# Attention and routed experts on one core: attention's transfers queued in written order, the routing noise later, and filler matmuls on TensorE

## The chip, the core and the metric

The kernel runs on one core of one Trainium2 chip. The metric is the device time of one execution in microseconds (us); lower is better. A core has five engines, each of which takes its own instructions strictly in the order in which they were queued: TensorE (PE, matmuls into PSUM; its weight loads are listed as PEld), VectorE (DVE), ScalarE (ACT), GpSimd (POOL) and SyncE (SP), which here issues nearly all transfers. The engines meet only at semaphores: an instruction whose input is not there stops everything queued behind it on its engine.

## What is computed

The program is a chain of three layers over 2304 tokens (4 sequences of 576) of width 512.

```python
# attention: q, k, v (4, 8, 576, 64); p (4, 8, 32, 64)
p_packed = softmax(p @ k.T / 8) @ v            # 32 packed rows for each sequence and head
x = softmax(q @ p_packed.T / 8) @ p_packed     # (2304, 512) after the heads are put together
# routing: 8 experts, two for each token
noisy = x @ w_gate + log1p(exp(x @ w_noise)) * noise
top2, weights = two_largest(noisy), softmax_of_the_two
# experts, d = 512, f = 1024
x2[token] = sum over its two experts of weight * (relu(x @ w1[e]) @ w2[e])
# dense layer, 512 -> 2048 -> 512
h = x2 @ w_in;  out = (h * sigmoid(h)) @ w_out
```

## The kernel before

The sequence of stages is attention (from 0 to about 118 us of the profile), then the eight experts, then the dense layer; from the first expert matmul on, TensorE has nearly always something to do.

**Attention** is worked off in 16 slots. `packed(b, g)` makes the packed rows of sequence `b` and head group `g` (eight units; `START1` gives the slot in which each begins), `unpacked(t, n, lg)` applies them to `n` token tiles of 128 rows from tile `t` on (ten units, u0 to u9; `START2`). Each unit is a generator of four steps, and `slot_steps` calls the steps that are due. In a unit of the first kind TensorE turns k (`kp`, `krp`), multiplies by p (`s`, L362 and L365), turns the exponentials (`ap`, `apr`) and multiplies by v (`pp`). In one of the second kind it turns q (`qp`), makes scores (`s`, L429 and L436), turns the normalised exponentials (`a2p`) and makes rows of x (`xp`), which ACT copies to `xr` and SP stores to DRAM (`xs`). The normalising multiplication (`sd` <- `sd`, `mx`) is GpSimd's, and stands between the exponentials and `a2p`.

**Routing** is done in two parts. `route(0, 11, ...)` takes the first 11 tiles as soon as u5 has made tile 10; it is a chain of small VectorE operations with two exchanges with ScalarE, and ends in `idx`, the list of the rows that expert 0 reads first. GpSimd fetches these rows with two indirect DMAs (`xg`, L196), TensorE turns them (`tps`), and the first expert matmul (`hps`, L208) follows. Tiles 11 to 17 (u6 to u9) are routed while expert 0 already computes.

**Weights of expert 0** are eight pieces (`wa0` to `wa7`) of 512 KB. Each is loaded to one of three buffers (`raws`), then `split` makes the two parts that the fast matmul format wants: ScalarE writes `wa?h`, GpSimd writes the remainder `wa?l` in four pieces.

```python
def split(hi, lo, src, eng=V):
    pin(A.activation(hi, src, AF.Copy))
    parts = 4 if eng is G else 1
    for i in range(parts):
        s = slice(i * 1024 // parts, (i + 1) * 1024 // parts)
        eng.tensor_tensor(lo[:, s], src[:, s], hi[:, s].bitcast(F32), op=OP.subtract)
```

**What sets the order.** The code is traced by a scheduler that orders each engine's instructions by its own estimate of when they can run, so an instruction may end up ahead of others that were written earlier; `tc.keep_in_program_order` takes that freedom away for the instructions given to it. The slot in which a piece of weights is asked for is `START1[i] + WLOAD` (slots 4, 5, 6, 7, 8, 8, 11 and 12), its split comes two slots later. SP has eight semaphores for its transfers, so a transfer is issued only when the eighth before it has landed.

Of the kernel before, what the change touches and what calls it, by code (L numbers as in the profile page):

```python
# [32 lines left out]
WLOAD = 4  # L33
# [11 lines left out]
def body(ctx: ExitStack, tc: tile.TileContext, q, k, v, p, wg, wn, noise, w1, w2, w_in, w_out, out):  # L45
# [58 lines left out]
    M = {"pin": False, "w": 384, "hb": 3}  # L104
# [26 lines left out]
    def load(dst, src, c, eng=V, runs=False):  # L131

        hi, lo = dst
        raw = raws.tile([P, 1024], F32, name="raw", tag="raw")
        if runs:
            for b in range(4):
                nc.sync.dma_start(raw[32 * b:32 * b + 32].rearrange("j (a f) -> j a f", a=4),
                                  src[b * P:(b + 1) * P].rearrange("(a j) f -> j a f", a=4))
        else:
            nc.sync.dma_start(raw.rearrange("p (c f) -> p c f", c=c), src.rearrange("(c p) f -> p c f", p=P))  # L140
        later.append(lambda: split(hi, lo, raw, eng))
# [93 lines left out]
    def expert_block(e, j0, n, x):  # L235
# [3 lines left out]
        def step2(f, h):  # L239
# [3 lines left out]
            if f == 7:  # L243
                for j, y in enumerate(acc[0]):
                    ysb = M["s"].tile([P, DM], F32, name="ysb", tag="ysb", bufs=3)
                    cp(A if j % 2 else V, ysb, y)
                    i = j0 + j
                    r0 = (e * TA + i if i < TA else E * TA + e * TB + i - TA) * P
                    nc.sync.dma_start(ys[r0:r0 + P, :], ysb)
# [8 lines left out]
    with ExitStack() as ax:  # L258
# [14 lines left out]
        def load_kv(nm, b, g):  # L273
            src = {"k": k, "v": v}[nm]
            m = wa.tile([P, 1024], F32, name=f"{nm}m", tag=f"wa{2 * b + g}{'hl'[nm == 'v']}")
            m = m.rearrange("p (h r) -> p h r", h=4)
            nc.sync.dma_start(m, src[b, 4 * g:4 * g + 4, 0:512, :].rearrange("h (p r) d -> p h (r d)", r=4))
# [6 lines left out]
        def load_q(b):  # L284
            for g in range(2):
                m = xp_.tile([P, 4 * BW], F32, name="qm", tag=f"x{'hl'[g]}{'ab'[b % 2]}")
                m = m[:, 0:1024].rearrange("p (h r) -> p h r", h=4)
                nc.sync.dma_start(m, q[b, 4 * g:4 * g + 4, 0:512, :].rearrange("h (p r) d -> p h (r d)", r=4))
# [4 lines left out]
            nc.sync.dma_start(qt["r", b // 2][o:o + 64], q[b, :, 512:576, :].rearrange("h p d -> p h d"))  # L293
# [12 lines left out]
        pd = sk.tile([P, 9, 64], F32, name="pd", bufs=1)  # L306
        nc.sync.dma_start(pd[:, 0:8, :], p.rearrange("b (g j) k d -> (j k) (b g) d", g=2))
# [6 lines left out]
        nc.sync.dma_start(wgn[0:64, :, 0:8], wg.rearrange("(h d) e -> d h e", h=H))  # L314
        nc.sync.dma_start(wgn[0:64, :, 8:16], wn.rearrange("(h d) e -> d h e", h=H))
# [25 lines left out]

        def packed(b, g):
# [66 lines left out]
        def unpacked(t, n, lg):  # L409
# [45 lines left out]
            for i in range(n):  # L455
# [11 lines left out]
                nc.sync.dma_start(xs[r0:r0 + P, :], xr)  # L467
# [184 lines left out]
        tick()  # L652
        r1 = route(EARLY, NT - EARLY, lgs[EARLY])
# [302 lines left out]
```

## Time and profile before

| what | value |
|---|---|
| time, median of 3 runs | 995.24 us (993.43 to 997.77) |
| the profiled execution's own time | 991.13 us |
| its span in the trace | 989.3 us |
| PE busy | 957.0 us, 97% of the span |
| PEld, DVE, ACT, POOL busy | 821.0, 447.4, 346.4, 313.4 us |
| chain that ended last | PE 90%, DVE 4%, DMA 3%, ACT 1% |

The span is what the trace covers; 1.8 us of the profiled execution lie around it. TensorE is busy nearly throughout, so what a change near the beginning is worth is the time by which it moves the point from which TensorE never waits again, and any matmul that it adds or speeds up.

### The profile page before, as it was taken

The numbers are of one execution on the slowest core, as the hardware profiler recorded it, in microseconds if no ns is written. First come the engines' busy times: TensorE is split into PE (matmuls) and PEld (weight loads), VectorE is DVE, ScalarE is ACT, GpSimd is POOL, SyncE is SP. The second block draws the span as 40 slices with busy tenths as digits, with TensorE's granted clock in tenths as the row PEclk, the third lists the DMA queues.
The fourth block names the chain that finished last, engine by engine and source line by source line (L and its number), as shares of the span: only waits on it lengthen the run. The fifth ranks groups of instructions, "written<-read, shape, count | busy, mean of one in ns | idle before, by whom it ended". The sixth has DMA issues, their size and how long they took to land.

```text
span 989.3 us, 14385 instructions
## 1 busy us (share of the span) xinstructions
PE 957.0 (97%) x5584; PEld 821.0 (83%) x5584; DVE 447.4 (45%) x871; ACT 346.4 (35%) x631; POOL 313.4 (32%) x345
## 2 busy tenths in 40 slices
PE   6989799999999999999999999999999999999996
PEld 4767589899999999998999988888888888888884
DVE  4537763666767576766634557222122221111111
ACT  3567322433434343433323343322222222222221
POOL 2166214343525243443200136333323322222221
PEclk9989899999999999999999999999999999999998
DMA  9994324576757676566623454111011110001001
GB/s 243 249 270 161 107 65 125 188 231 202 231 167 227 188 235 199 189 226 207 188 64 117 149 194 136 54 28 37 22 53 33 32 43 1 1 1 43 0 1 46
DMA packets 82298, 122.49 MB, mean 124 GB/s; under 512 B 16432, under 2 KB 49200, under 8 KB 82224
## 3 DMA queue, kind: packets, MB, share of 16 engines
q1 hardware_dynamic: 74704, 101.58, 32.6%
q0 software_dynamic: 7520, 19.93, 7.0%
q8 instruction: 46, 0.75, 0.3%
q14 instruction: 28, 0.23, 0.1%
HBM read 93.17 MB, written 28.31 MB: 123 GB/s over the span
## 4 chain that ended last, share of the span: by engine, by line
PE 90%; DVE 4%; DMA 3%; ACT 1%; SPq 1%; issue 1%; ACTq 0%
PE hps L208 14%; PE hps L210 14%; PE hps L209 14%; PE acc L219 14%; PE acc L218 14%; PE acc L220 14%; PE xp L460 1%; PE tps L157 1%; PE s L429 1%; PE s L362 1%; DMA vm<-in_v_dram 1%; DMA km<-in_k_dram 1%; DVE rt_oa L534 1%; PE kp L351 0%; DMA raw<-wf_out 0%
## 5 line engine op out<-in xcount | busy, mean ns | idle before, releaser
L176 POOL DMA_INDIRECT xg<-xs,idx x120 | 127.0, 1059 | 195.1 <-DVE xturn L185 147.6
L750 POOL TENSOR_TENSOR gl<-sg,gh 128x512 fp32r<-128x512 f32 (+1 forms) x80 | 95.4, 1194 | 253.5 <-ACT gh L749 237.9
L231 ACT ACTIVATE hh<-hps 128x384 fp32r<-128x384 f32 (+1 forms) x128 | 56.0, 438 | 260.5 <-PE hps L210 256.8
L746 DVE TENSOR_TENSOR sg<-hps,sg 128x512 f32<-128x512 f32 (+1 forms) x80 | 50.7, 634 | 196.2 <-ACT sg L745 196.0
L232 DVE SCALAR_TENSOR_TENSOR hl<-hps,hh 128x384 fp32r<-128x384 f32 (+1 forms) x128 | 62.4, 488 | 122.0 <-ACT hh L231 121.3
L745 ACT ACTIVATE sg<-hps 128x512 f32<-128x512 f32 (+1 forms) x80 | 44.2, 553 | 189.5 <-PE hps L210 189.2
L749 ACT ACTIVATE gh<-sg 128x512 fp32r<-128x512 f32 (+1 forms) x80 | 47.1, 589 | 79.3 <-DVE sg L746 79.1
L736 POOL DMA_INDIRECT y<-ys,slots x36 | 36.7, 1019 | 110.9 <-DVE hl L232 72.4
L739 DVE TENSOR_SCALAR y<-y,gates 128x512 f32<-128x512 f32 x18 | 10.9, 607 | 37.9 <-DMA y<-ys,slots 37.9
L740 DVE SCALAR_TENSOR_TENSOR y<-y,gates,y 128x512 f32<-128x512 f32 x18 | 15.7, 871 | 25.1 <-DMA y<-ys,slots 25.0
L460 PE MATMUL xp<-ppBD,a2T 128*128 128x272 f32 (+1 forms) x80 | 23.5, 433 | 1.6 <-ACT xr L51 0.8
L185 DVE STREAM_TRANSPOSE xturn<-xg 128x512 f32<-128x512 f32 x30 | 21.2, 706 | 3.7 <-DMA wf_in<-t 2.5
L689 DVE SCALAR_TENSOR_TENSOR t<-raw,t 128x512 int32<-128x512 int32 x32 | 22.2, 693 | 0.9
L690 DVE SCALAR_TENSOR_TENSOR t<-raw,t 128x512 int32<-128x512 int32 x32 | 22.1, 691 | 0.9
L196 POOL DMA_INDIRECT xg<-xs,idx x10 | 9.7, 969 | 40.3 <-DVE idx_f L555 19.5
L686 ACT ACTIVATE t<-raw 128x512 f32<-128x512 f32 x32 | 21.2, 662 | 0.1
L208 PE MATMUL hps<-xha,wa3h 128*128 128x256 f32 (+1 forms) x56 | 17.7, 316 | 1.8 <-DVE sg L746 1.8
L160 DVE TENSOR_TENSOR xla<-tps,xha 128x512 fp32r<-128x512 f32 x14 | 9.6, 690 | 21.1 <-ACT xha L159 21.1
L53 DVE COPY ysb<-acc 128x512 f32<-128x512 f32 x24 | 16.4, 682 | 4.9 <-PE acc L220 4.8
L429 PE MATMUL s<-ppT,qT 128*128 128x64 f32 x128 | 17.9, 291 | 0.0
L208 PE MATMUL hps<-xha,wa0h 128*128 128x256 f32 (+1 forms) x56 | 17.6, 314 | 0.2 <-ACT xha L159 0.2
L208 PE MATMUL hps<-xha,wa2h 128*128 128x256 f32 (+1 forms) x56 | 17.7, 316 | 0.1
(450 smaller groups left out, 2976.4 us busy)
## 6 DMA issues: line engine op xcount, KB each, us to landing
raw<-in_moe_w_dram SPq DMA_DIRECT2D x56, 512.0 KB, 4.0
ys<-ysb SPq DMA_DIRECT2D x40, 256.0 KB, 3.7
raw<-in_moe_w_in_dram SPq DMA_DIRECT2D x16, 512.0 KB, 4.3
raw<-in_moe_w_out_dram SPq DMA_DIRECT2D x16, 512.0 KB, 4.1
xs<-xr SPq DMA_DIRECT2D x18, 256.0 KB, 2.1
km<-in_k_dram SPq DMA_DIRECT2D x8, 512.0 KB, 7.6
vm<-in_v_dram SPq DMA_DIRECT2D x8, 512.0 KB, 7.6
qm<-in_q_dram SPq DMA_DIRECT2D x8, 512.0 KB, 7.1
```

The lines of the kernel that those rows point to most:

```text
L176: G.indirect_dma_start(out=xg[:, g * P:(g + 1) * P], out_offset=None, in_=xs[:, :].rearrange("n (a f) -> (n a) f", a=4), in_offset=bass.In ...
L208: T.matmul(ps, wh[:, c, s], xh[:, c, :n], start=c == 0, stop=False)
L209: T.matmul(ps, wh[:, c, s], xl[:, c, :n], start=False, stop=False)
L210: T.matmul(ps, wl[:, c, s], xh[:, c, :n], start=False, stop=c == 3)
L218: T.matmul(y, hh[:, s], wh[:, f % 2, :], start=f == 0, stop=False)
L219: T.matmul(y, hh[:, s], wl[:, f % 2, :], start=False, stop=False)
L220: T.matmul(y, hl[:, s], wh[:, f % 2, :], start=False, stop=f == last)
L231: A.activation(hh, ps, AF.Relu)
L232: V.scalar_tensor_tensor(hl, ps, 0.0, hh.bitcast(F32), op0=OP.max, op1=OP.subtract)
L746: V.tensor_tensor(sg, ps, sg, op=OP.mult)
L749: A.activation(gh, sg, AF.Copy)
L750: G.tensor_tensor(gl, sg, gh.bitcast(F32), op=OP.subtract)
```

## The change

There are four edits. First, every transfer of attention that was issued with `nc.sync.dma_start` now goes through a helper `dma` that keeps it in program order on SP, until the second routing part (`M["queue"] = False`). The written order is changed a little for it: the remainders `vr` of the last sequence are loaded after all else of it (`load_kv` is cut in two, `load_main` and `load_rest`), and these remainders have four buffers and not three. Second, the noise is asked for in slot 8 and not in slot 4. Third, the weights of expert 0 are asked for in slots 6 to 13 (`WSLOT`) and not in slots 4 to 12, and behind the stores of attention's rows that were written before them; the tile `pd` (p) takes one of the three `raws` buffers at the start. Fourth, 28 matmuls of 128x128 by 128x512 in bf16 that write an unused PSUM tile (`junk`, all ones) are put on TensorE, in program order: 10 ahead of everything, 3 before p is turned, 5 after it, 5 after the first unit's scores and 5 after slot 1.

```diff
-WLOAD = 4
+WSLOT = (6, 7, 8, 9, 10, 11, 12, 13)
+NOISE = 8
...
+    def dma(dst, src):
+        ins = nc.sync.dma_start(dst, src)
+        if M["queue"]:
+            tc.keep_in_program_order(ins)
...
-            r = sk.tile([REST, 4, 64], F32, name=f"{nm}r", bufs=3)
-            nc.sync.dma_start(r, src[b, 4 * g:4 * g + 4, 512:576, :].rearrange("h p d -> p h d"))
-            kv[nm, b, g] = (m, r)
+            kv[nm, b, g] = [m]
+
+        def load_rest(nm, src, b, g):
+            r = sk.tile([REST, 4, 64], F32, name=f"{nm}r", bufs=4)
+            dma(r, src[b, 4 * g:4 * g + 4, 512:576, :].rearrange("h p d -> p h d"))
+            kv[nm, b, g].append(r)
...
+        junk = pS2[0].tile([P, 4, P], F32, name="junk", tag="s2")
+
+        def idle(n):
+            for _ in range(n):
+                tc.keep_in_program_order(T.matmul(junk, ones, ones[:, None, :].to_broadcast([P, 4, P]), start=True, stop=True))
...
+            if b + g == 0:
+                idle(5)
...
+        idle(10)
         M["delay"] = 2
...
-                    load_kv("v", b, g)
+                    load_kv("v", b, g, 1 if b == 3 else 2)
+                for g in range(2 if b == 3 else 0):
+                    load_kv("v", b, g, 0)
...
-            if slot == 4:
+            if slot == NOISE:
                 load_noise()
             slot_steps(slot)
             if slot == 0:
+                idle(3)
                 turn_p()
+            if slot < 2:
+                idle(5)
             tick()
-            for i, s0 in enumerate(START1):
-                if slot == s0 + WLOAD:
+            for i, s0 in enumerate(WSLOT):
+                if slot == s0:
...
+        M["queue"] = False
         r1 = route(EARLY, NT - EARLY, lgs[EARLY])
```

The scheduler answers with another order on the other engines too. On ScalarE, in the middle of attention, these rows stood behind the turned exponentials of u0 (`a2T`); `a1T` belongs to the sixth packed unit, `xr` to tiles 0 and 1:

```order
L51 ACTIVATE a2T_799<-a2p 128x512
L115 ACTIVATE wa0h<-raw 128x1024
L51 ACTIVATE a1T<-ap 128x512
L51 ACTIVATE ppBD_181<-wp 128x16
L51 ACTIVATE xr<-xp 128x2x4x32
L51 ACTIVATE a1T<-ap 128x512
L442 ACTIVATE sd_912<-sd_912 128x512
L51 ACTIVATE xr<-xp 128x2x4x32 x2
L115 ACTIVATE wa1h<-raw 128x1024
```

and these stand there now:

```order
L52 ACTIVATE a2T_806<-a2p 128x512
L52 ACTIVATE ppBD_181<-wp 128x16
L52 ACTIVATE a1T<-ap 128x512
L465 ACTIVATE sd_919<-sd_919 128x512
L52 ACTIVATE xr<-xp 128x2x4x32
L52 ACTIVATE a1T<-ap 128x512
L52 ACTIVATE xr<-xp 128x2x4x32
L52 ACTIVATE qT<-qp 128x512
L52 ACTIVATE xr<-xp 128x2x4x32 x2
L52 ACTIVATE qT<-qp 128x512 x2
L52 ACTIVATE a2T_976<-a2p 128x512
```

The two weight copies are gone from this place; `wa0h` comes after the first copy of tile 3, `wa1h` after those of tile 4. At the end of u5, where routing begins (`rt_sa` is routing's exponential and logarithm), ScalarE had

```order
L51 ACTIVATE a1T<-ap 128x512
L51 ACTIVATE xr<-xp 128x2x4x32 x2
L51 ACTIVATE a2T_1462<-a2p 128x512
L51 ACTIVATE qT<-qp 128x512
L51 ACTIVATE xr<-xp 128x2x4x32 x2
L51 ACTIVATE qT<-qp 128x512
L480 ACTIVATE rt_sa_1326<-rt_sa_1326 128x88
L51 ACTIVATE qT<-qp 128x512
L481 ACTIVATE rt_sa_1326<-rt_sa_1326 128x88
L51 ACTIVATE qT<-qp 128x512
L51 ACTIVATE ppT_195<-tp 64x4x32 x2
```

and has now

```order
L52 ACTIVATE a1T<-ap 128x512
L121 ACTIVATE wa2h<-raw 128x1024
L52 ACTIVATE a2T_1477<-a2p 128x512
L52 ACTIVATE xr<-xp 128x2x4x32 x2
L503 ACTIVATE rt_sa_1337<-rt_sa_1337 128x88
L52 ACTIVATE qT<-qp 128x512 x2
L504 ACTIVATE rt_sa_1337<-rt_sa_1337 128x88
L52 ACTIVATE qT<-qp 128x512 x2
L52 ACTIVATE ppT_195<-tp 64x4x32 x2
L121 ACTIVATE wa3h<-raw 128x1024
L52 ACTIVATE ppBD_193<-wp 128x16
L601 ACTIVATE rt_ex_1642<-rt_ex_1642 128x11
```

with the loads that these copies wait for standing thus on SP (the rows before `xs` are the noise; the four `xs` are tiles 4 to 7, the three are 8 to 10; `raw` is a piece of weights, here `wa2`, `wa3` and `wa4`):

```order
L108 DMA xs<-xr 128x512 x4
L108 DMA raw<-in_moe_w_dram 32x4x256 x4
L108 DMA xs<-xr 128x512 x3
L108 DMA raw<-in_moe_w_dram 32x4x256 x4
L108 DMA raw<-in_moe_w_dram 128x2x512
```

Before, all eight pieces had been asked for before tile 9 was stored. The third place is GpSimd from the end of the first routing part on (`sd_1586` was u7's, `sd_1645` u8's and `sd_1663` u9's normalising multiplication; now they are `sd_1596`, `sd_1660` and `sd_1678`). It had

```order
L119 TENSOR_TENSOR wa7l<-raw,wa7h 128x256 x4
L396 COPY ppBD_197<-px 32x64 x4
L446 TENSOR_TENSOR sd_1586<-sd_1586,mx_1584 128x512
L196 DMA xg<-xs,idx_102 128x512 x2
L446 TENSOR_TENSOR sd_1645<-sd_1645,mx_1643 128x512
L446 TENSOR_TENSOR sd_1663<-sd_1663,mx_1661 128x256
L196 DMA xg<-xs,idx 128x512 x8
```

and has now

```order
L125 TENSOR_TENSOR wa4l<-raw,wa4h 128x256 x4
L202 DMA xg<-xs,idx_102 128x512 x2
L469 TENSOR_TENSOR sd_1596<-sd_1596,mx_1594 128x512
L125 TENSOR_TENSOR wa5l<-raw,wa5h 128x256 x4
L125 TENSOR_TENSOR wa6l<-raw,wa6h 128x256 x4
L469 TENSOR_TENSOR sd_1660<-sd_1660,mx_1658 128x512
L469 TENSOR_TENSOR sd_1678<-sd_1678,mx_1676 128x256
L125 TENSOR_TENSOR wa7l<-raw,wa7h 128x256 x4
L202 DMA xg<-xs,idx 128x512 x8
```

u7's multiplication went from ahead of the fetch to behind it, and the remainders of `wa5` and `wa6` stand ahead of u8's. On TensorE the order around this place is unchanged in what matters: the `a2p` of u8 and u9 and two `xp` of u8 stand ahead of `tps`, and `tps` ahead of the first `hps`. From the second expert on the orders of all engines are the same as before.

## Rows read from the trace of the kernel before

**Rows 1.** Windows: start:end, length, busy PE, PEld, DVE, ACT, POOL, PEclk, DMA share, GB/s
```profile
0.00:20.00 20.00, 12.50 (x93) 8.02 (x97) 7.60 (x24) 5.64 (x10) 5.40 (x25) 1.00 0.88 231
...
50.00:61.30 11.30, 8.37 (x74) 6.82 (x72) 3.55 (x12) 5.85 (x12) 4.95 (x7) 0.70 1.09 257
61.30:90.00 28.70, 28.14 (x276) 21.18 (x273) 15.37 (x53) 23.98 (x55) 18.07 (x31) 1.00 0.78 237
90.00:110.00 20.00, 13.23 (x199) 10.43 (x198) 19.63 (x92) 7.17 (x21) 8.71 (x17) 0.89 0.29 94
...
118.40:500.00 381.60, 380.51 (x2188) 343.42 (x2189) 249.32 (x446) 143.92 (x248) 134.64 (x128) 1.00 0.59 189
```

**Rows 2.** Timeline, PE: start, us, line, what, count, idle before and its releaser
```profile
5.08 1.94 PE L351 MATMUL kp<-ident,km 128*128 128x128 f32 x8 [5.08 <-DMA km<-in_k_dram]
...
20.87 1.09 PE L351 MATMUL kp<-ident,km 128*128 128x128 f32 x8
...
37.66 0.63 PE L351 MATMUL kp<-ident,km 128*128 128x128 f32 x4
```

**Rows 3.** The tile km, only its transfer issued at 29.88 us
```profile
DMA to landing us min/median/max: 7.6/7.6/7.6
```

**Rows 4.** Timeline, ACT, in the middle of attention
```profile
51.98 1.06 ACT L115 ACTIVATE wa0h<-raw 128x1024 fp32r<-128x1024 f32 x1 [3.29 <-DMA raw<-in_moe_w_dram]
```

**Rows 5.** Timeline, PE, in the middle of attention
```profile
53.57 0.66 PE L377 MATMUL ap<-ident,a 128*128 128x128 f32 x4 [2.93 <-ACT a1T L51]
...
54.52 3.47 PE L429 MATMUL s<-ppT,qT 128*128 128x64 f32 x16
...
63.33 0.60 PE L451 MATMUL a2p<-ident,sd 128*128 128x128 f32 x4
...
71.07 2.00 PE L429 MATMUL s<-ppT,qT 128*128 128x64 f32 x16
```

**Rows 6.** DMA issues up to 130 us: count, KB each, median us to landing
```profile
xs<-xr SPq DMA_DIRECT2D x18, 256.0 KB, 2.1
...
raw<-in_moe_w_dram SPq DMA_DIRECT2D x24, 128.0 KB, 3.1
```

**Rows 7.** Timeline, ACT, before the routing and behind it
```profile
85.04 0.39 ACT L51 ACTIVATE xr<-xp 128x256 f32<-128x256 f32 x1
...
105.23 0.60 ACT L51 ACTIVATE a2T<-a2p 128x512 f32<-128x512 f32 x1 [3.70 <-PE a2p L451]
```

**Rows 8.** Timeline, DVE, the first routing part
```profile
89.82 0.25 DVE L478 TENSOR_TENSOR rt_w<-lg 128x88 f32<-128x88 f32 x1
...
92.76 0.66 DVE L488 TENSOR_TENSOR rt_sp<-rt_sp,rt_h 128x88 f32<-128x88 f32 x1
...
94.16 0.25 DVE L492 TENSOR_TENSOR rt_ny<-rt_sp,nzt 128x88 f32<-128x88 f32 x1
...
98.42 0.68 DVE L439 TENSOR_REDUCE mx<-s 128x16 f32<-128x512 f32 x1
...
109.70 0.17 DVE L544 TENSOR_SCALAR idx<-idx_f 128x2 int32<-128x2 f32 x1
```

**Rows 9.** Timeline, POOL, around the first routing part
```profile
91.14 2.86 POOL L119 TENSOR_TENSOR wa6l<-raw,wa6h 128x256 fp32r<-128x256 f32 x4 [5.03 <-PE pp L388]
...
103.43 1.05 POOL L446 TENSOR_TENSOR sd<-sd,mx 128x512 f32<-128x512 f32 x1 [4.29 <-DVE rt_lo L523]
...
110.79 1.15 POOL L196 DMA_INDIRECT xg<-xs,idx  x1 [6.32 <-PE s L436]
...
113.22 1.05 POOL L446 TENSOR_TENSOR sd<-sd,mx 128x512 f32<-128x512 f32 x1
```

**Rows 10.** Timeline, PE, up to the first expert matmuls
```profile
114.33 0.66 PE L451 MATMUL a2p<-ident,sd 128*128 128x128 f32 x4 [0.93 <-POOL sd L446]
...
118.43 0.38 PE L208 MATMUL hps<-xha,wa0h 128*128 128x256 f32 x1 [0.24 <-ACT xha L159]
...
122.76 0.40 PE L218 MATMUL acc<-wa4h,hh 128*128 128x512 f32 x1
```

More of the change, by code (lines that the diff above doesn't have):

```diff
@@ L102, in body @@
     few = const.tile([P, E], F32)
-    M = {"pin": False, "w": 384, "hb": 3}
+    M = {"pin": False, "w": 384, "hb": 3, "queue": True}
+    def dma(dst, src):
+        ins = nc.sync.dma_start(dst, src)
+        if M["queue"]:
+            tc.keep_in_program_order(ins)
     def pin(ins):
@@ L136, in load @@
             for b in range(4):
-                nc.sync.dma_start(raw[32 * b:32 * b + 32].rearrange("j (a f) -> j a f", a=4),
+                dma(raw[32 * b:32 * b + 32].rearrange("j (a f) -> j a f", a=4),
                                   src[b * P:(b + 1) * P].rearrange("(a j) f -> j a f", a=4))
         else:
-            nc.sync.dma_start(raw.rearrange("p (c f) -> p c f", c=c), src.rearrange("(c p) f -> p c f", p=P))
+            dma(raw.rearrange("p (c f) -> p c f", c=c), src.rearrange("(c p) f -> p c f", p=P))
         later.append(lambda: split(hi, lo, raw, eng))
@@ L248, in step2 @@
                     r0 = (e * TA + i if i < TA else E * TA + e * TB + i - TA) * P
-                    nc.sync.dma_start(ys[r0:r0 + P, :], ysb)
+                    dma(ys[r0:r0 + P, :], ysb)
         for f in range(8):
@@ L270, in body, with load_kv, load_main @@
         kv = {}
-        def load_kv(nm, b, g):
+        def load_kv(nm, b, g, part=2):
             src = {"k": k, "v": v}[nm]
+            if part:
+                load_main(nm, src, b, g)
+            if part != 1:
+                load_rest(nm, src, b, g)
+        def load_main(nm, src, b, g):
             m = wa.tile([P, 1024], F32, name=f"{nm}m", tag=f"wa{2 * b + g}{'hl'[nm == 'v']}")
             m = m.rearrange("p (h r) -> p h r", h=4)
-            nc.sync.dma_start(m, src[b, 4 * g:4 * g + 4, 0:512, :].rearrange("h (p r) d -> p h (r d)", r=4))
-            r = sk.tile([REST, 4, 64], F32, name=f"{nm}r", bufs=3)
-            nc.sync.dma_start(r, src[b, 4 * g:4 * g + 4, 512:576, :].rearrange("h p d -> p h d"))
-            kv[nm, b, g] = (m, r)
+            dma(m, src[b, 4 * g:4 * g + 4, 0:512, :].rearrange("h (p r) d -> p h (r d)", r=4))
+            kv[nm, b, g] = [m]
[3 more added lines that the diff above has]
+            kv[nm, b, g].append(r)
         qt = {}
@@ L292, in load_q @@
             o = 64 * (b % 2)
-            nc.sync.dma_start(qt["r", b // 2][o:o + 64], q[b, :, 512:576, :].rearrange("h p d -> p h d"))
+            dma(qt["r", b // 2][o:o + 64], q[b, :, 512:576, :].rearrange("h p d -> p h d"))
         nzt = one.tile([P, NT, E], F32)
@@ L299, in load_noise @@
                 t0 = 9 * (b // 2) + 4 * (b % 2)
-                nc.sync.dma_start(nzt[:, t0:t0 + 4, :],
+                dma(nzt[:, t0:t0 + 4, :],
                                   noise[b * S:b * S + 512, :].rearrange("(p r) e -> p r e", r=4))
-                nc.sync.dma_start(nzt[64 * (b % 2):64 * (b % 2) + 64, 9 * (b // 2) + 8, :],
+                dma(nzt[64 * (b % 2):64 * (b % 2) + 64, 9 * (b // 2) + 8, :],
                                   noise[b * S + 512:(b + 1) * S, :])
         load_kv("k", 0, 0)
-        pd = sk.tile([P, 9, 64], F32, name="pd", bufs=1)
-        nc.sync.dma_start(pd[:, 0:8, :], p.rearrange("b (g j) k d -> (j k) (b g) d", g=2))
+        pd = raws.tile([P, 1024], F32, name="pd", tag="raw")[:, 0:576].rearrange("p (c d) -> p c d", d=64)
+        dma(pd[:, 0:8, :], p.rearrange("b (g j) k d -> (j k) (b g) d", g=2))
         load_kv("v", 0, 0)
@@ L313, in body @@
         G.memset(wgn[64:P], 0.0)
-        nc.sync.dma_start(wgn[0:64, :, 0:8], wg.rearrange("(h d) e -> d h e", h=H))
-        nc.sync.dma_start(wgn[0:64, :, 8:16], wn.rearrange("(h d) e -> d h e", h=H))
+        dma(wgn[0:64, :, 0:8], wg.rearrange("(h d) e -> d h e", h=H))
+        dma(wgn[0:64, :, 8:16], wn.rearrange("(h d) e -> d h e", h=H))
         pT = sk.tile([P, 9, 2, P], F32, name="pT", bufs=1)
@@ L466, in unpacked @@
                 r0 = (t + i) * P
-                nc.sync.dma_start(xs[r0:r0 + P, :], xr)
+                dma(xs[r0:r0 + P, :], xr)
             yield
```

2 lines of the change are left out of this document (1 added, 1 removed).

## The prediction

> **What bounds the kernel now.** I read the windows first, to see which engine is full in which stretch [rows 1]. From 118.4 us on TensorE is busy for 380.51 of 381.60 us, so all that follows is passed on one to one: the change is worth the shift of the first expert matmul, which stands at 118.43 [rows 10], and the few matmuls that change sides of it. Ahead of it there are four stretches with different limits. In the first 20 us TensorE works 12.50 us and the transfers are busy for 0.88 of the time: data bounds. From 61.3 to 90 TensorE works 28.14 of 28.70 us: it bounds, and the reader is to see that ScalarE with 23.98 us is not far behind. Between them, from 50 to 61.3, TensorE has only 8.37 us at a granted clock of 0.70, that is mostly at the lower of its two levels. From 90 to 110 VectorE has 19.63 us of 20: the routing chain bounds.
>
> Then I followed the waits and the timelines. The hole at 50 us is ScalarE's: `wa0h` waited 3.29 us for its transfer [rows 4], `a1T` stood behind it, and TensorE waited 2.93 us for that [rows 5]. The routing part runs from 89.82 to 109.87 (0.17 us behind 109.70) [rows 8], GpSimd fetches at 110.79 [rows 9], and the first `hps` stands at 118.43 [rows 10], 8.56 us behind the list. These three spans are what the change moves.
>
> **The fillers and the start.** At the lower level eight transposes take 1.94 us, at the upper one 1.09 [rows 2]; the granted clock shows 1.00 over the first 20 us [rows 1], but these durations say otherwise. The nearest row for a filler is an expert matmul of 512 columns with 0.40 us from start to end [rows 10]; 28 of them are at most 11.2 us, of which ten lie in the 5.08 us in which TensorE waits for k anyhow [rows 2], the others in the idle 2.4 us and in place of work that waits for data. What TensorE gains there it cannot keep: the second k of sequence 2 is issued at 29.88 and lands 7.6 us later, at 37.5 [rows 3], and TensorE needs it at 37.66 [rows 2]. The order on SP up to it is as before but for one small remainder. So the start gives 0.2 us; the bounds are 0 and 1 us, one reordered piece of work being done ahead of that wait.
>
> **The hole at 50 us.** ScalarE no longer meets weights there, so the 2.93 us go, and with them the fall of the clock: from 53.57 on sixteen score matmuls took 3.47 us, at 71.07 the same sixteen took 2.00 [rows 5]. The low level lasts to about 61.3 [rows 1], and 7.7 us of work at 1.74 times its price are 4.4, a gain of 3.3. Together 6.2 us at the `a2p` at 63.33 [rows 5]. Bounds: 2.9, if the clock falls anyhow, and 7. What could be late next is q of sequence 2, which u5 needs; but it is now queued right behind k and v, ahead of weights and noise, and lands several us before.
>
> **What ScalarE waits for now.** The weights are not gone; they moved behind the stores on SP. `wa2h` stands behind the store of tile 7, whose last `xr` ended at 85.43 [rows 7]; store, four issues and 3.1 us of landing [rows 6] put its data some 5.5 us after that, while ScalarE reaches it about 3.5 us after it. Queued behind it are `rt_sa` and the last `xr` of u5. VectorE has some operations to do before it needs `rt_sa`, so of 2 us I count 1.0. `wa3h` stands behind the stores of tiles 8 to 10 and holds up `rt_ex`, on which VectorE's next operations wait: 0.6 more. `wa1h`, behind the stores of tiles 2 and 3, stops ScalarE for about a microsecond at a time when TensorE bounds: 1.0. Together 2.6 us lost; bounds 0 (TensorE and VectorE always have something in hand) and 6 (each of four waits as long as `wa0h`'s 3.29 and half of that on the path).
>
> **The routing chain.** VectorE had three 512-column operations of u7 and two of u8 in it; now it has two in all. Three times 0.68 us [rows 8] would be 2.0, but some of them filled waits for TensorE: I take 1.2. Against this, remainders run on GpSimd while the chain runs. Before, these were `wa6l` and `wa7l`; while `wa6l` ran, an operation of 88 columns took 0.66 us, and 0.25 us when it had ended [rows 8, 9]. Now `wa3l` and `wa4l` lie there, and `wa4l` later, beside the longest operations. I take 0.5 us; bounds 0 and 2.9, the length of one remainder.
>
> The Trainium skill says in "SBUF — State Buffer", section "Who interferes with whom", that a DVE instruction with two SBUF inputs and a GpSimd instruction that reads SBUF shut each other out for a whole instruction. By that rule a two-input operation of VectorE that meets `wa4l` would wait for the whole piece; the 0.66 against 0.25 agrees with it, but says 0.4 for each operation met. What it would make of the time is the rival below.
>
> So the list is ready 0.2 + 6.2 + 1.2 - 2.6 - 0.5 = 4.5 us earlier.
>
> **From the list to the first expert matmul.** Here the change costs. u7's multiplication (1.05 us [rows 9]) now waits for the fetches; before it was done at 103.43, in front of them. The fetches end 3.35 us after the list (113.22 against 109.87 [rows 8, 9]), u7's multiplication at 4.4, its `a2p` and `a2T` (0.66 and 0.60 [rows 7, 10]) at 5.7, and only then comes `wa5h` on ScalarE (1.06 [rows 4]), at 6.8. GpSimd meets `wa5l` and `wa6l` ahead of u8's multiplication: twice 2.8 us [rows 9], so that it starts 12.4 us after the list and not 3.35. Behind it, in TensorE's order, wait the `a2p` of u8 and u9, two `xp`, `tps` and every expert matmul. From u8's multiplication to `hps` it took 5.2 us (118.43 less 113.22); nothing in that part gets shorter. So `hps` comes 9.0 us later against the list. The bounds: 7.5, as before part of the 5.2 us was a wait for the fetched rows, now long there; 11, if the transfers of `wa5` and `wa6`, asked for behind the store of tile 12, are late too. One `xp` more is done ahead of `hps` (0.4 us saved), and TensorE, idle for longer, may start the experts at the lower level (0.5 lost).
>
> **Sum.** -4.5 + 9.0 + 0.1 = +4.6 us. The profiled execution of 991.13 us would become 995.7. The median of the runs is 4.1 us above the profiled execution, so I add the shift to it: 995.24 + 4.6 = 999.8, say 999.5.
>
> **The rivals.**
> - *The waits for weights are free.* If TensorE bounds so firmly that ScalarE's waits never reach it, and GpSimd's remainders cost VectorE nothing, the list is 7.6 us earlier, and with the lower bound of 7.5 for the last part nothing is left: -0.1 us, 995. For it speaks that ScalarE has six copies of 1.06 us [rows 4] less in the middle (`wa2h` to `wa7h` leave it); against it, that `wa0h`'s wait did reach TensorE within 2 us.
> - *The chain ahead of the list shrinks enough.* This one ends faster. The price of GpSimd's order is fixed to the list; it decides from the point where the list is 14 us earlier, near 96 us. From 61.3 to 110 TensorE is idle for 7.3 us [rows 1]; were all of it gone with the 6.2 us and the 1.2, the list would be 14.7 us earlier and the time 990. Against it stands that VectorE is full for 19.63 of 20 us in that stretch, and most of its work stays.
> - *The weights come later still.* If each load on SP waits for its store and the store for ScalarE, the waits add up to the upper bounds: the list gains 1 us, the last part costs 10.5, and the time is 1005.
> - *VectorE is shut out.* If every two-input operation beside `wa4l` stands until the remainder has ended, one whole remainder of 2.86 us [rows 9] is lost and not 0.5: 2.4 more, 1002. Against it stands that `wa6l` lay beside the chain for as long and operations were slowed by 0.4, not stopped. This is the Trainium skill's rule from above, and has the same sign as my sum.
> - *The fillers do nothing.* That is in the sum: they are worth 0.2 us, and 0 if the clock stays low.
>
> **How the numbers follow.** My sum has 0.50, VectorE shut out 0.08 (together 0.58), and its own range is +1 to +8 us; free waits 0.20; the weights later still 0.08; faster 0.14. A change of this kernel below 0.5%, 5 us, cannot be told from none. The sum's case lies below and above that line in about equal parts, so slower has 0.29 + 0.07 = 0.36, the same 0.29 + 0.20 + 0.01 = 0.50, faster 0.14. The range reaches from 991.5, into the rivals below, to 1005.5, which holds the later weights; a fifth is left out.
>
> **What would show it.** In the profile of the changed kernel: no wait of `a1T` near 50 us and a full clock from 50 to 61; `a2p` of u1 near 57; waits of ScalarE for `raw` at `wa1h`, `wa2h` or `wa3h`; the list near 105; `wa5l` and `wa6l` back to back on GpSimd ahead of u8's multiplication, some 12 us after the list; `hps` near 122 to 123. I am wrong if the list comes before 100 us, or if u8's multiplication starts within 6 us of it.

## The result

The changed kernel takes 1006.52 us (median of 5 runs, 1005.2 to 1009.34) against 995.24: a ratio of 1.0114, 95% interval 1.0091 to 1.0138. It is slower by 11.3 us; the forecast was 999.5 with a range from 991.5 to 1005.5, and the time lies above it. The profiled execution took 1005.2 us, span 1003.0. In the runs further down three single executions, of 1.9, 2.4 and 3.1 ms, are left out of the ratios.

The windows of the changed kernel, in the stretches of [rows 1] (the fourth is the one from the end of the routing chain to the first expert matmul):

```profile
50.00:61.30 11.30, 11.16 (x167) 9.05 (x167) 6.62 (x21) 6.03 (x15) 2.89 (x9) 1.00 0.59 179
61.30:90.00 28.70, 23.42 (x217) 16.57 (x213) 13.68 (x52) 18.42 (x47) 11.11 (x15) 1.00 0.44 132
90.00:110.00 20.00, 12.44 (x139) 9.66 (x132) 17.07 (x76) 6.99 (x18) 10.44 (x18) 0.76 0.24 80
110.00:129.40 19.40, 15.36 (x68) 10.94 (x67) 7.42 (x22) 8.94 (x18) 12.97 (x17) 0.55 0.67 221
129.40:500.00 370.60, 368.76 (x2130) 332.46 (x2130) 243.25 (x436) 139.34 (x240) 133.00 (x128) 1.00 0.60 190
```

The reader is to see three things. From 50 to 61.3 TensorE is now busy for 11.16 us at full clock, where it had 8.37 at 0.70: the hole is gone. But from 61.3 to 90, where it had been full (28.14 of 28.70), it has 23.42, and from 110 to 129.4 its clock is 0.55. From 129.4 on it is full again, so what counts is the first expert matmul.

TensorE's timeline at the points of [rows 2, 5, 10]:

```profile
20.82 1.06 PE L372 MATMUL kp<-ident,km 128*128 128x128 f32 x8 [1.72 <-DMA km<-in_k_dram]
...
56.66 0.66 PE L474 MATMUL a2p<-ident,sd 128*128 128x128 f32 x4
...
62.80 0.72 PE L483 MATMUL xp<-ppBD,a2T 128*128 128x272 f32 x2 [1.08 <-ACT xr L52]
...
77.03 0.72 PE L483 MATMUL xp<-ppBD,a2T 128*128 128x272 f32 x2 [1.18 <-ACT xr L52]
...
123.82 1.54 PE L474 MATMUL a2p<-ident,sd 128*128 128x128 f32 x6 [1.41 <-POOL sd L469]
...
129.38 0.38 PE L214 MATMUL hps<-xha,wa0h 128*128 128x256 f32 x1
```

`hps` stands at 129.38 and not at 118.43 [rows 10]: 10.95 us later. The other 2.75 us between the two profiled spans lie behind it, 1.4 of them where the experts end and the dense layer begins: TensorE waited 3.2 us there and not 1.8. In the profiles of this study that wait was 1.8 or 1.9 us in the four kernels that cost nothing (before, e7, e11 and e13 below) and 2.8 to 4.1 in all others; why is not known. The medians differ by 11.3 us, less than the profiled spans, since the profile of before is of an execution 4.1 us faster than its median.

The three spans of the forecast then read so. The `a2p` of u1 came at 56.66, 6.67 us earlier than [rows 5]. The routing chain began at 86.42, only 3.40 us earlier than [rows 8], and ended at 110.02, 0.15 us later. From there to `hps` it took 19.36 us and not 8.56. VectorE's timeline of the chain:

```profile
86.42 0.25 DVE L501 TENSOR_TENSOR rt_w<-lg 128x88 f32<-128x88 f32 x1
...
90.22 0.35 DVE L414 TENSOR_SCALAR px<-pp,mx 128x128 f32<-128x128 f32 x1 [1.19 <-PE pp L411]
...
97.12 0.55 DVE L602 TENSOR_SCALAR rt_dn<-rt_ex 128x11 f32<-128x11 f32 x1 [1.88 <-ACT rt_ex L601]
...
102.03 0.70 DVE L593 TENSOR_SCALAR rt_late<-rt_rr 128x22 f32<-128x22 f32 x1
...
104.94 0.70 DVE L595 TENSOR_TENSOR rt_up<-rt_up,rt_late 128x22 f32<-128x22 f32 x1
...
105.65 3.29 DVE L557 TENSOR_TENSOR rt_oa<-iota_lo,rt_lo 128x768 f16<-128x768 f16 x4
...
109.85 0.17 DVE L567 TENSOR_SCALAR idx<-idx_f 128x2 int32<-128x2 f32 x1
```

Two waits of more than 1 us stand in it (1.19 and 1.88 us), and two operations on 22 columns that took 0.70 us each. What ScalarE waited for between 50 and 100 us (total us, times, longest):

```profile
ACT xr L52 <- DMA xs<-xr: 4.1, 2, 2.8
ACT wa3h L121 <- DMA raw<-in_moe_w_dram: 3.4, 1, 3.4
...
ACT wa1h L121 <- DMA raw<-in_moe_w_dram: 1.7, 1, 1.7
ACT wa2h L121 <- DMA raw<-in_moe_w_dram: 1.3, 1, 1.3
...
ACT wa0h L121 <- DMA raw<-in_moe_w_dram: 0.9, 1, 0.9
```

The list holds what the forecast counted (weights) and what it did not: two waits for a store, 4.1 us together, because the buffer of `xr` was not free. TensorE's waits of 1.08 and 1.18 us at `xp`, shown above, came right behind them. GpSimd's timeline at the end of the chain and behind it, which answers to [rows 9]:

```profile
101.09 4.51 POOL L125 TENSOR_TENSOR wa4l<-raw,wa4h 128x256 fp32r<-128x256 f32 x4
...
112.40 0.95 POOL L202 DMA_INDIRECT xg<-xs,idx  x1 [0.31 <-issue]
113.37 1.05 POOL L469 TENSOR_TENSOR sd<-sd,mx 128x512 f32<-128x512 f32 x1
117.25 2.78 POOL L125 TENSOR_TENSOR wa5l<-raw,wa5h 128x256 fp32r<-128x256 f32 x4 [2.82 <-ACT wa5h L121]
119.98 2.77 POOL L125 TENSOR_TENSOR wa6l<-raw,wa6h 128x256 fp32r<-128x256 f32 x4
122.71 1.62 POOL L469 TENSOR_TENSOR sd<-sd,mx 128x512 f32<-128x512 f32 x2
```

u7's multiplication follows the fetch, `wa5l` and `wa6l` stand ahead of u8's, which starts 12.69 us behind the list (12.4 were forecast). ScalarE's timeline shows why `wa5l` starts no earlier: `wa5h` stands behind the `a2T` of u7, and this waited for u7's `a2p`.

```profile
115.63 0.60 ACT L52 ACTIVATE a2T<-a2p 128x512 f32<-128x512 f32 x1 [5.10 <-PE a2p L474]
116.12 1.05 ACT L121 ACTIVATE wa5h<-raw 128x1024 fp32r<-128x1024 f32 x1
```

And the chain that ended last, in its pieces between 60 and 96 us (start, us, what; four of the longest pieces):

```profile
60.49 4.48 DMA raw<-in_moe_w_dram
...
68.87 3.09 DMA raw<-in_moe_w_dram
...
83.63 3.28 DMA raw<-in_moe_w_dram
...
91.03 4.62 DMA raw<-in_moe_w_dram
```

Four times the chain passes through a load of weights (4.48, 3.09, 3.28 and 4.62 us), that is `wa0` to `wa3`. The chain also names the load of `wa5`, which landed at 114.72, 2.5 us ahead of `wa5l`; by the rows above it was `wa5h` that `wa5l` waited for. Over the whole span transfers have 4% of this chain, where they had 3%.

### The profile page after: what moved, and what is told of

Read it like the earlier page. It is cut to its first block, busy times and chain, and to the rows that moved or that the text cites. A ratio compares the mean times of both kernels' runs of the same rounds, so it can differ in the third digit from the quotient of the medians.

```text
span 1003.0 us, 14432 instructions
## 1 busy us (share of the span) xinstructions
PE 966.4 (96%) x5612; PEld 824.7 (82%) x5612; DVE 448.6 (45%) x871; ACT 346.0 (34%) x631; POOL 314.6 (31%) x345
## 4 chain that ended last, share of the span: by engine, by line
PE 87%; DMA 4%; SPq 2%; DVE 2%; ACT 2%; issue 2%; POOL 1%; ACTq 0%; POOLq 0%; DVEq 0%
PE hps L214 14%; PE hps L215 14%; PE hps L216 14%; PE acc L224 14%; PE acc L225 13%; PE acc L226 13%; SPq L108 2%; DMA raw<-in_moe_w_dram 2%; PE tps L163 1%; PE xp L483 1%; PE s L452 1%; DMA ys<-ysb 1%; DMA km<-in_k_dram 1%; PE s L383 1%; DMA y<-ys,slots 1%
## 5 line engine op out<-in xcount | busy, mean ns | idle before, releaser
L483 PE MATMUL xp<-ppBD,a2T 128*128 128x272 f32 (+1 forms) x80 | 27.1, 482 | 4.9 <-ACT xr L52 4.2
L483 PEld LDWEIGHTS xp<-ppBD,a2T 128*128 128x128 f32 (+1 forms) x80 | 13.6, 213 | 11.0 <-ACT xr L52 7.7
L452 PEld LDWEIGHTS s<-ppT,qT 128*128 128x128 f32 x128 | 18.1, 218 | 0.9 <-DVE sd L464 0.4
```

The costliest lines, as they stand in the source:

```text
L483: T.matmul(xp[sl], aT[:, 2 * i + g, sl], ppBD[b, g], start=True, stop=True)
```

## The experiments

The runs came in four groups, each on one chip. The kernel before took 995.3 (e1 to e4), 1004.2 (e5 to e8), 994.4 (e9 to e12) and 1005.0 us (e13 and e14) on them, so only ratios to it compare across groups. Points of time come from one profile each and scatter by some microseconds: e3, which changes nothing ahead of the list, had the chain begin 3.0 us later than the changed kernel.

| run | ratio to before, 95% interval |
|---|---|
| changed kernel | 1.0114 (1.0091 to 1.0138) |
| e1: without fillers | 1.0097 (1.0077 to 1.0118) |
| e2: queue free | 1.0055 (1.0037 to 1.0074) |
| e3: remainders behind u8 and u9 | 1.0072 (1.0046 to 1.0099) |
| e4: two buffers for `qr` | 1.0097 (1.0074 to 1.0119) |
| e5: before + 28 fillers | 1.0041 (1.0021 to 1.0060) |
| e6: before + strict order | 1.0101 (1.0076 to 1.0125) |
| e7: before + later weights | 0.9999 (0.9981 to 1.0018) |
| e8: stores on ScalarE | 1.0059 (1.0040 to 1.0078) |
| e9: e8 + route cleared | 1.0062 (1.0039 to 1.0084) |
| e10: e9 without fillers | 1.0048 (1.0033 to 1.0064) |
| e11: before + route cleared | 0.9979 (0.9967 to 0.9990) |
| e12: e5 + 4 fillers | 1.0032 (1.0019 to 1.0045) |
| e13: before + first 10 fillers | 1.0008 (0.9992 to 1.0024) |
| e14: before + other 18 | 1.0023 (1.0009 to 1.0037) |

**e1, the change without its fillers.**

```diff
         def idle(n):
-            for _ in range(n):
-                tc.keep_in_program_order(T.matmul(junk, ones, ones[:, None, :].to_broadcast([P, 4, P]), start=True, stop=True))
+            pass
```

> The changed kernel without its 28 fillers, the rest of the change as it is. My theory: the time is lost in the wait between the list of rows and the first expert matmul and in stores that came late, and the fillers lie where TensorE waits for data anyhow. Then this run is within 2 us of the changed kernel, 1005 to 1008, the list near 110 and the first expert matmul near 129. Rival: the fillers themselves are the loss. 28 of them at 0.40 us are 11.2 us, which is just the 11.3 us lost; then this run is at 995 to 997.

1005.51 us: the 11.2 us of the fillers are not the loss. The list and `hps` did not come where they were expected: they stood at 117.46 and 138.00. That profile is of the slowest of the five executions, 1011.84 us, so its points of time say little of the median.

**e2, the change with a free queue.**

```diff
-    M = {"pin": False, "w": 384, "hb": 3, "queue": True}
+    M = {"pin": False, "w": 384, "hb": 3, "queue": False}
```

> The changed kernel with the transfers not held in program order; later slots for weights and noise, four buffers for the remainders of k and v, and the fillers stay. My theory: the strict queue is what makes stores and weights late and thereby puts GpSimd's remainders wa5l and wa6l ahead of u8's multiplication; with it gone the list is at 106 to 110, the first expert matmul 8 to 9 us behind it, and the time 990 to 996. Rival: asking for weights later is what costs, whatever the queue does; then the time stays above 1003.

1000.41 us, half of the loss. GpSimd's order at the end of the chain is that of before again, and `hps` stands 8.68 us behind the list (114.29, 122.97), about as it had with 8.56. But the list did not come at 106 to 110. Another wait took the place of the old one, ScalarE's and behind it TensorE's. First ScalarE's timeline (start, us, engine and line, what, the idle time before and what ended it):

```profile
61.42 1.06 ACT L121 ACTIVATE wa2h<-raw 128x1024 fp32r<-128x1024 f32 x1 [3.52 <-DMA raw<-in_moe_w_dram]
```

And TensorE's, in the same run, at its first work behind that wait:

```profile
63.01 1.11 PE L372 MATMUL kp<-ident,km 128*128 128x128 f32 x4 [3.46 <-ACT qT L52]
```

So asking late alone did not remove the hole: with a free queue a piece of weights, now the third, meets ScalarE in the middle of attention again, some 9 us later than the first had [rows 4].

**e3, the change with GpSimd's order mended.**

```diff
-            G.tensor_tensor(sd, sd, mx[:, 2, :, None].to_broadcast([P, 8 * n, 32]), op=OP.mult)
+            turn = G.tensor_tensor(sd, sd, mx[:, 2, :, None].to_broadcast([P, 8 * n, 32]), op=OP.mult)
+            if t == 17:
+                M["turn"] = turn.ins
...
+        held = []
...
+                    if i >= 5:
+                        held.append(later.pop())
...
+        with tc.issue_after(M["turn"]):
+            for fn in held:
+                fn()
```

> The changed kernel, with wa5l, wa6l and wa7l queued on GpSimd behind the multiplications of u8 and u9; nothing ahead of the list is changed. My theory: u8's multiplication starts 4 to 5 us behind the list and not 12.7, the first expert matmul stands 11 to 12 us behind the list and not 19.4, and the time is 998 to 1000. Rival: GpSimd's order is hidden behind TensorE's own work at the lower clock and ScalarE's copies; then at most 2 us come back, 1004 to 1006.

1002.51 us, 4.0 us less than the changed kernel, where 6.5 to 8.5 were expected: between the two theories. `hps` stood 14.50 us behind the list (112.40, 126.90), 4.9 less than in the changed kernel. u8's multiplication came 9.2 us behind the list, not 4 to 5: GpSimd waited for its exponentials, not for remainders.

```profile
115.74 1.07 POOL L469 TENSOR_TENSOR sd<-sd,mx 128x512 f32<-128x512 f32 x1
121.64 1.05 POOL L469 TENSOR_TENSOR sd<-sd,mx 128x512 f32<-128x512 f32 x1 [4.83 <-ACT sd L465]
```

In front of these stand u7's transposes and the scores of u9, at the lower clock, and `wa5h` on ScalarE. So of the 10.8 us that `hps` lost against the list the remainders hold 4.9, and u7's multiplication behind the fetch, by these rows, most of the rest; no run moved it alone.

**e4, two buffers for qr.** In the changed kernel SP stood for 8.1 us at the third `qr`, from 45.6 on, with two q, a `qr`, and then all stores and weights behind it:

```profile
44.45 1.15 SPq L108 DMA_DIRECT2D qm<-in_q_dram  x2
53.70 0.61 SPq L108 DMA_DIRECT2D qr<-in_q_dram  x1
...
57.33 1.04 SPq L108 DMA_DIRECT2D xs<-xr  x2
```

```diff
-                qt["r", b // 2] = sb.tile([P, 8, 64], F32, name="qr", bufs=1)
+                qt["r", b // 2] = sb.tile([P, 8, 64], F32, name="qr", bufs=2)
```

> The changed kernel with two buffers for the remainders of q (qr) and not one, so that the third qr on SP need not wait from 45.6 to 53.7 us for the first one to be read, with two q pieces, another qr, all stores and all weights of expert 0 queued behind it. My theory: this stop is what made the stores late (ScalarE waited 2.83 us for a buffer of xr) and the weights wa0 and wa1 (0.92 and 1.72 us); the first store is issued near 52 and not 57.3, the list is 3 to 5 us earlier, near 106, and the time 1001 to 1003. Rival: the weights are late because of their slots, and the stores because of the 512 KB transfers beside them; then the list stays at 109 to 110 and the time at 1005 to 1007.

1005.78 us. The stop was gone (`qr` issued at 48.49, the first stores at 53.87), and with it ScalarE's waits for stores; but ScalarE still waited 2.5 us at `wa3h` and 0.9 to 1.5 at `wa0h` to `wa2h`, and the time was the same. The list came at 115.18, later than either theory said: the chain began at 86.61 and took 28.6 us. My theory fell here. The stop was plain to see, and removing it brought nothing in the time.

**e5 to e7, the edits one by one on the kernel before.** e5 has the 28 fillers alone (the ten at the beginning and the four groups of 3 and 5 in the waits). e6 has the strict order: the changed kernel with the slots and the place of the noise of before, and `idle` empty; the written order, the four buffers and the place of `pd` come with it. e7 has the later weights alone, asked for at the slots of the change. In e5 (the helper `idle` is that of the change):

```diff
+            if b + g == 0:
+                idle(5)
...
+        idle(10)
...
             if slot == 0:
+                idle(3)
                 turn_p()
+            if slot < 2:
+                idle(5)
```

In e6, against the changed kernel (`idle` is emptied as in e1):

```diff
-WSLOT = (6, 7, 8, 9, 10, 11, 12, 13)
-NOISE = 8
+WSLOT = (4, 5, 6, 7, 8, 8, 11, 12)
+NOISE = 4
```

In e7:

```diff
-WLOAD = 4
+WSLOT = (6, 7, 8, 9, 10, 11, 12, 13)
...
-            for i, s0 in enumerate(START1):
-                if slot == s0 + WLOAD:
+            for i, s0 in enumerate(WSLOT):
+                if slot == s0:
```

> The kernel before with the 28 fillers alone. With the free queue 5.1 us of the loss stayed. My theory: the fillers are worth nothing on either side, since TensorE, faster at the start, waits longer for the k of sequence 1 near 21 us; then this run is at 994 to 997. Rival: they cost, because TensorE comes to that wait earlier and its clock falls in it; then most of the 5.1 us is here, 998 to 1000.

> The kernel before with the strict order of transfers alone (the written order and the four buffers of the remainders with it): weights and noise in the slots of before, no fillers. My theory: the strict order by itself makes stores wait behind loads and loads behind stores, and puts wa6l and wa7l ahead of u8's multiplication on GpSimd; the time is 1000 to 1004, the first expert matmul 14 us or more behind the list. Rival: only the later slots do harm, and a strict order that asks early is as good as before; then 993 to 997.

> The kernel before with the weights of expert 0 asked for in the later slots 6 to 13, alone (noise still in slot 4, free queue, no fillers). GpSimd's order at the end of the first routing part is that of before, so the first expert matmul stands 8.5 to 9 us behind the list. If the later slots hold the 5.1 us that the free queue left (ScalarE met a transfer again, wa2h waited 3.52 us, and TensorE 3.46 behind it), this run is at 999 to 1001. If they belong to the fillers or the noise, it is at 994 to 997.

The strict order costs 1.01%, nearly as much as the whole change. Its `hps` stood 16.10 us behind the list (115.34, 131.44), since GpSimd had `wa6l` ahead of the fetch and `wa7l` ahead of u8's multiplication:

```profile
115.56 2.78 POOL L125 TENSOR_TENSOR wa6l<-raw,wa6h 128x256 fp32r<-128x256 f32 x4 [6.38 <-ACT wa6h L121]
118.51 1.15 POOL L202 DMA_INDIRECT xg<-xs,idx  x1 [0.17 <-issue]
...
120.94 2.75 POOL L125 TENSOR_TENSOR wa7l<-raw,wa7h 128x256 fp32r<-128x256 f32 x4
123.66 1.61 POOL L468 TENSOR_TENSOR sd<-sd,mx 128x512 f32<-128x512 f32 x2
```

It also loses on a path that the changed kernel does not have: TensorE waited 2.42 us, up to 57.64, for a q that was issued behind noise and weights. The later slots cost nothing (0.9999). The fillers cost 0.41%, where I had expected nothing; e13 and e14 come back to that.

**e8, the stores off SP.**

```diff
-                dma(xs[r0:r0 + P, :], xr)
+                nc.scalar.dma_start(xs[r0:r0 + P, :], xr)
```

> The changed kernel with attention's stores issued by ScalarE and not by SP, so that neither a load stands behind a store nor a store behind a load; slots, strict order of the loads and fillers stay. My theory: weights behind stores are the cause. Then wa2h and wa3h no longer wait (1.29 and 3.37 us), only wa7l stands ahead of the fetch on GpSimd, the list comes at 104 to 107, the first expert matmul 9 to 11 us behind it, and the time is 992 to 997. Rival: the later slots or the fillers cost by themselves, and ScalarE's 18 more issues add to it; then 1003 or more.

1.0059: half of the loss again. Weights no longer stand behind stores, the remainders up to `wa5l` are done before the route (but the waits at `wa2h` and `wa3h`, which were to go, are still 1.4 and 1.2 us), and `hps` stood 8.56 us behind the list, just as before. But the chain took 24.12 us (89.32 to 113.44), in part because `wa7l` ran beside its longest operations. VectorE's timeline of e8:

```profile
106.96 5.41 DVE L557 TENSOR_TENSOR rt_oa<-iota_lo,rt_lo 128x768 f16<-128x768 f16 x4
```

GpSimd's, in the same microseconds:

```profile
106.87 4.95 POOL L125 TENSOR_TENSOR wa7l<-raw,wa7h 128x256 fp32r<-128x256 f32 x4
```

The four `rt_oa` took 5.41 us and not 3.29 as in the changed kernel, where GpSimd had ended, and the remainder itself took 4.95 and not 2.8: each delays the other. Alone the two take 3.29 and 2.78 us, 6.07 together; side by side they filled the 5.50 us from 106.87 to 112.37. The Trainium skill ("SBUF — State Buffer", section "Who interferes with whom") says that a VectorE instruction with two inputs in SBUF and a GpSimd instruction that reads SBUF contend for a pair of ports which one of them holds for its whole instruction; a remainder is four instructions of 0.7 us, and these rows agree with turns of about that length. In the changed kernel the operations on 22 columns at 102.03 and 104.94 took about 0.5 us longer each, beside `wa4l`. The edit of e8 may have a price of its own, too: ScalarE, which now issues the stores itself, stood idle from 59.62 until it issued one at 63.83.

**e9 and e10, the route cleared, with and without fillers.** `wa6l` and `wa7l` are held behind u9's multiplication as in e3 (`i >= 6`), on top of e8.

> The run with the stores on ScalarE, and in addition wa6l and wa7l queued on GpSimd behind the multiplication of u9, so that no remainder runs beside the routing chain. There the four operations of rt_oa took 5.41 us beside wa7l, and 3.28 us in the kernel before with GpSimd idle; rt_oc, rt_up and rt_lo were longer by some 1.5 us. My theory: remainders beside the chain cost it 3 to 4 us; the chain from rt_w to the list takes 20 to 21 us and not 24.1, and the ratio to the kernel before falls from 1.0059 to about 1.002. Rival: VectorE does not wait for GpSimd, the chain is longer for other reasons (TensorE at the lower clock); then the chain stays at 23 to 24 us and the ratio at 1.005 to 1.007.

> The same kernel without the 28 fillers. On the free queue the fillers cost 0.41%, on the strict one 0.17%, both with intervals of 0.2%. If they cost by themselves, this run is 0.2 to 0.4% below the one with them, at 0.998 to 1.000 of the kernel before; if what was seen there belongs to the single order, both are the same within 0.1%. Under 0.998 it would beat both kernels.

In e9 the chain took 20.81 us, 3.3 less than in e8, and `rt_oa` 3.29:

```profile
92.75 0.25 DVE L503 TENSOR_TENSOR rt_w<-lg 128x88 f32<-128x88 f32 x1
...
109.20 3.29 DVE L559 TENSOR_TENSOR rt_oa<-iota_lo,rt_lo 128x768 f16<-128x768 f16 x4
...
113.39 0.17 DVE L569 TENSOR_SCALAR idx<-idx_f 128x2 int32<-128x2 f32 x1
```

So remainders beside the chain do cost it what was expected. But the ratio did not move, where 1.002 was expected: the chain began 3.4 us later, at 92.75, behind a wait of ScalarE for a store (2.68 us at 89.88). One profile cannot say whether that goes with holding the remainders. Without fillers (e10) the ratio was 1.0048, less than e9's, but within its interval, and above the 0.998 to 1.000 of the theory that the fillers cost by themselves.

**e11, the route cleared in the kernel before.**

```diff
+                    if i >= 6:
+                        held.append(later.pop())
```

(with the rest of e3's edit)

> The kernel before with wa6l and wa7l queued on GpSimd behind the multiplication of u9; nothing else is changed. There they lie at 91 to 98 us beside the short operations of the chain. By the theory that remainders cost the chain time they cost least there: operations of 88 columns took 0.66 us instead of 0.25 for about four of them, so 1 to 1.5 us come back, ratio 0.998 to 0.999. If VectorE does not wait for GpSimd, 0.9995 to 1.0005.

0.9979 (0.9967 to 0.9990): faster than both kernels. The chain took 18.46 us instead of 20.05:

```profile
91.72 0.25 DVE L480 TENSOR_TENSOR rt_w<-lg 128x88 f32<-128x88 f32 x1
...
93.95 0.25 DVE L490 TENSOR_TENSOR rt_sp<-rt_sp,rt_h 128x88 f32<-128x88 f32 x1
...
110.01 0.17 DVE L546 TENSOR_SCALAR idx<-idx_f 128x2 int32<-128x2 f32 x1
```

`rt_sp`, which had taken 0.66 beside `wa6l` [rows 8], took 0.25. The profile does not show how the gain reaches the end: the chain began 1.9 us later in it, and `hps` stood at 118.83.

**e12 to e14, where the fillers cost.** e12 adds four fillers ahead of the first work on sequence 1; e13 has the first ten alone, with the order of before on ScalarE, VectorE, GpSimd and SP; e14 the other 18. What e12 has more than e5:

```diff
+            if (b, g) == (1, 0):
+                idle(4)
```

All that e13 has:

```diff
+        idle(10)
```

> The kernel before with the 28 fillers and 4 more ahead of TensorE's work on sequence 1, so that part of its wait of 1.73 us for the k of that sequence is filled. In the profile of the run with 28 the granted clock was 0.67 and 0.65 from 20 to 30 us, behind that wait, and the eight kp behind it still took 1.06 us. My theory: what the fillers cost is this fall; with the wait halved the clock stays and the ratio is 0.999 to 1.001. Rival: the cost lies elsewhere (more fillers, more cost); then 1.004 or more.

> The kernel before with the first ten fillers alone; on every engine all else stands in the order of before. The ten lie in the 5.08 us in which TensorE waits for the first k, and end at 5.2 us; what they can change is the clock behind them. Theory A: the fillers' price is the work that they push back and the order that the scheduler makes around them; then these ten cost nothing, ratio 0.999 to 1.001. Theory B: the price is the clock: TensorE, faster from 5 us on, waits at 19 to 21 us for the k of sequence 1 and its clock falls there; then the ten cost as much as the 28, ratio 1.002 to 1.004. In both nothing is gained: by 20.9 us TensorE is no further than before.

> The kernel before with the 18 later fillers (3, 5, 5 and 5) and not the first ten. Theory A (pushed back work and another order): the price is here, ratio 1.002 to 1.004, and a wait of ScalarE for weights or of TensorE for q is seen in the middle that the kernel before does not have. Theory B (the clock behind the first wait): at most 1.002.

e12 told nothing: k landed later in its profiled execution, the wait at 21.16 was as long as in e5 (1.69 and 1.73 us), and the ratio lies between the two theories. The first ten cost nothing that can be measured (1.0008), the other 18 cost 0.23%. In e14 and in e5 TensorE waits for copies of q where it did not before. TensorE's timeline of e14:

```profile
61.96 0.65 PE L430 MATMUL qp<-ident,qm 128*128 128x128 f32 x4 [2.02 <-ACT qT L51]
...
65.20 1.09 PE L459 MATMUL a2p<-ident,sd 128*128 128x128 f32 x4 [1.50 <-ACT qT L51]
```

The same of e5:

```profile
60.06 0.66 PE L430 MATMUL qp<-ident,qm 128*128 128x128 f32 x4 [1.16 <-ACT qT L51]
...
62.66 1.09 PE L459 MATMUL a2p<-ident,sd 128*128 128x128 f32 x4 [0.85 <-ACT qT L51]
```

ScalarE had just waited 3.28 and 1.34 us (e14) for `wa1` and `wa2`. In e14 these waits are part of the price: with one of 1.54 us ahead of them they make 5.06 us, where e13, in the same group, has a single wait of 3.08 (at 52.92), and the `a2p` of u1 stands 2.43 us later than in e13, `hps` 3.24. In e5 they are not: with one of 0.98 us ahead of them they make 2.99, no more than the 2.93 of before [rows 5], the `a2p` of u1 stands at 62.66, earlier than before, and ScalarE's order up to `hps` is that of the kernel before. So the order that the scheduler makes around the fillers does not explain e5. e13's interval reaches to 0.24% and e5 had 0.41: a part of the price may lie in the clock. What the fillers cost by stays open.

## Why the prediction was wrong

- **The hole: right.** 6.2 us were forecast at u1's `a2p`, 6.67 measured, with the clock at 1.00.
- **The start: right that nothing is gained; whether it is free stays open.** TensorE reached the eight `kp` of sequence 1 at 20.82 us, against 20.87 [rows 2], after a wait of 1.72 that it had not had: what the fillers gained went into waiting for k. I had not looked for a price of the fillers; alone they cost 0.41% (e5), in the changed kernel 0.17% with intervals that overlap (e1).
- **"Together 2.6 us lost; bounds 0 and 6": the step that failed first.** Of the 2.6 us only 1.0, that of `wa1h`, was counted ahead of the route; but of the 6.67 us 3.27 were gone by its start. I had counted ScalarE's waits for three weights and put those for stores, 4.1 us in two, at nothing. A store had to wait for its turn on SP behind loads while `xr` had few buffers; the waits that TensorE had right behind (1.08 and 1.18 us) are 2.26 of the 3.27. I had named the loads that stand behind stores, but not the stores that stand behind loads. The size is not firm: in e4, without waits for stores, 1.91 us were lost on this stretch, in e3, with the code of the changed kernel up to there, 5.12.
- **The routing chain: the step that failed next.** I took 1.2 us of gain, 0.5 of loss beside remainders and 1.6 of waits; that is 0.9 us longer. The chain took 3.55 us longer (23.60 against 20.05). VectorE stood still for 4.03 us of it, against 0.25 before, and 3.07 of that are the two waits behind `wa2h` and `wa3h`. Its busy time was nearly the same, 19.57 against 19.80, though three operations of 0.68 had left: other operations took longer beside the remainders, the two on 22 columns 1.1 us together, twice the 0.5 of the sum. By the busy time the remainders cost some 1.8 us (an estimate: 2.0 less 0.2), between the 0.5 of the sum and the 2.9 of the rival in which VectorE is shut out.
- **From the list to `hps`: the mechanism right, the size too small.** 9.0 us were forecast, 10.8 measured. u8's multiplication came at 12.69 (12.4 forecast); from it to `hps` it took 6.67 us where I had kept 5.2, since TensorE was at the lower clock (0.50 from 110 to 126 us): six `a2p` took 1.54 us, where four had taken 0.66 [rows 10]. I had given 0.5 us for that.
- **All that follows is passed on one to one: not quite.** 2.75 us of the 13.7 between the two profiled spans lie behind `hps`, where I had put nothing.
- **The sum.** List 0.15 us later and not 4.5 earlier: 4.65 us off. The last part 1.8 more. 4.6 + 4.65 + 1.8 is 11.05, less 0.1 for the small terms 10.95. The nearest rival, in time and in kind, was that of the weights that come later still (1005), to which I gave 0.08. Neither sign that was to show me wrong came: both guarded against a list that is early or a u8 that is early, and what I had too small was lateness.

Which edit did it: the strict order. Letting the queue go returns about 0.6% (e2), so does taking only the stores off it (e8). Without fillers the strict order costs 1.0% whether weights and noise are asked for late (e1, 1.0097) or early (e6, 1.0101), so the later slots add nothing to it, and alone they cost nothing (e7); the late noise had no run of its own. The stop at `qr` is innocent too (e4). The 0.55% that is left in e2 agrees within the intervals with the 0.41% that the fillers cost alone (e5). The prices do not add up (1.01 and 0.41 against 1.14 for all), and e10, without fillers and with the stores off SP, still costs 0.48%, which no run explains.

## What to carry to other kernels

When loads and stores share one queue that keeps the written order, count both directions: loads that wait behind a store, and stores that wait behind a load and then hold the buffer that the next copy needs. How much the second direction cost here is not settled, as e4 removed these waits and gained nothing. Follow the piece that comes late through every engine that will touch it: here a late piece of weights became a late remainder, and this stood in front of the one multiplication for which all waited. Long operations of GpSimd are best kept away from a chain of short ones on VectorE; that alone shortened the chain by 1.6 us and made the kernel before 0.2% faster (e11).

## What the runs showed of the hardware

Fillers did raise TensorE's clock: the first eight `kp` took 1.07 us and not 1.94 [rows 2], from 5.2 us on. It can fall again behind one short wait: in e5 the four `ap` at 22.10, 1.4 us behind a wait of 1.73, took 1.11 us (granted clock 0.67 from 20 to 25 us); in the changed kernel, behind a wait of 1.72, they took 0.66. Two waits of the same length had different ends, and in the kernel without fillers of e7 a wait of 3.35 left the eight `kp` at 1.97, while in e3, with fillers, one of 2.87 left them at 1.07. The clock in such a place is thus not to be counted on either way.
